# A sparse attention with a mixture of experts: the last 64 keys' products with V on four quarter tiles, no scaling of q on ScalarE, and a new order of all operations, gating and first fetches

## The chip, the cores and the metric

The kernel runs on one NeuronCore of a Trainium2 chip. The metric is the device time of one execution in microseconds. Engines are named as in the profile: PE is TensorE, PEld its weight load, DVE is VectorE, ACT is ScalarE, POOL is GpSimd, SP is SyncE, which issues nearly all DMAs.

## The reference

Attention over 8 batches of 8 heads with 576 positions of 64 elements keeps, in each row, only the scores that lie within tau of the row's maximum. Its output goes through a noisy gate that sends each of 4608 tokens to two of eight experts. All is in 32-bit floats.

```python
scores = q @ k.T / sqrt(64)                       # 576 x 576 for each head
thresh = max(scores, -1) - tau
scores = where(scores >= thresh, scores, -1e9)
attn = exp(scores - max(scores, -1)); attn /= sum(attn, -1) + 1e-9
x = rows of (attn @ v), 4608 x 512
noisy = x @ w_gate + log1p(exp(x @ w_noise)) * noise
two largest of noisy per token -> weights by softmax over the two
out[token] += weight * relu(x @ w1[e]) @ w2[e]    # 512 -> 1024 -> 512
```

## The kernel before

The attention goes by *pairs* of heads, 32 of them, four to a batch; two heads of 64 elements fill the 128 partitions. For a pair there are nine tiles of scores: eight of 128 rows (four for each head) and one, number 0, with the last 64 rows of both heads. A tile passes five stations: `scores` (L305, PE; each operand is split in a high and a low part, hi and lo), `rowmax` (L316, DVE: scores by minus 1/8 to SBUF, with the row's extreme), `exponent` and `threshold` (L322, L330, ACT), `mask` (L344, DVE: keeps what lies under the threshold and adds up the row), `ptile` (L356, PE transposes) and `pcopy` (L364, ACT, PSUM to SBUF). `prem` and `pcorner` turn what belongs to the last 64 keys into the tile ptr.

`avpiece` (L432) multiplies by V. The output of a pair is made in two pieces of 320 and 256 columns (`PIECES`), each in a bank of its own; head s goes to partitions 64 s to 64 s + 63. For keys 0 to 511 a product takes 128 rows and 64 columns of the array, for the last 64 keys (kt = 4) 64 rows and 64 columns. `oev` (L438) copies a piece, `xlpart` (L451, L452) turns it and multiplies it by the gate's weights, `xev` (L465) scales it to xr.

Before its scores a pair's q and k are made ready: `scale_q` (L224, ACT) multiplies q by 1 or 0 as tau is not negative or is, `split` (L234 ACT, L235 POOL) makes hi and lo, and `spread` (L256, SP) copies them within SBUF to where the two heads need them; qd holds the last 64 rows of q (L251, POOL). `norm` and `invert` (L400 to L411) make the reciprocal of the row sums, mostly on POOL.

After every fourth pair comes the *gating* of a batch: `gate_sum` (t, t, lgs on POOL), `gate_abs` (ab, DVE), exponential and logarithm on ACT, `gate_soft` to `gate_soft2` on POOL with one DVE reciprocal, `gate_max` (five maxima and five index searches on DVE), `gate_hot`, `gate_rank` (PE), `gate_slot` and ten `gate_put`, each an indirect DMA of POOL to slot_table. For the last batch but one and the last this runs beside the start of the first expert (`Experts.start`): tokens and index from the table, gathers of rows (L973, POOL), a bounce through DRAM (L983), loads (L993), and the first layers (L1023).

Nothing is reordered on the chip. Each engine runs its instructions in the order in which the program recorded them and waits on semaphores. That order is set by tables of times: `at` files each call under a time, and the calls are then made in order of time. A pair is nine units long. `TIMES` gives each station of a pair its time from the pair's start (S scores, R rowmax, E, H threshold, M mask, T, P, A products with V by piece and key tile, O, X, V; values over 9 fall beside later pairs), `LAST` what differs for the last two pairs, `GATES` and `PUTS` the gating, `START` the first expert. PSUM has two double banks for scores (sp) and four banks (tp) for all else in the attention, taken in turn.

Of the kernel before, what the change touches and what calls it, by code (L numbers as in the profile page):

```python
# [79 lines left out]

TIMES = dict(
    S=(-0.9, 2.24, 2.9, 3.76, 4.09, 5.17, 5.5, 6.47, 8.21),
    R=(-0.03, 2.79, 3.44, 3.87, 4.41, 5.93, 6.26, 7.12, 8.86),
    E=(0.94, 3, 4.74, 6.37, 6.91, 7.02, 9.4, 10.16, 10.38),
    H=(1.27, 0, 4.3, 0, 5.39, 0, 7.45, 0, 9.62),
    M=(1.7, 4.96, 5.06, 6.58, 7.56, 7.88, 9.83, 10.81, 11.68),
    T=(2.14, 5.61, 12.22, 12.33, 13.2, 13.63, 13.85, 15.15, 15.69),
    P=(2.57, 6.8, 13.52, 12.65, 14.28, 14.82, 14.71, 16.23, 16.99),
    A=((17.53, 18.18, 17.32, 18.29, 19.92),
       (19.05, 17.64, 18.08, 17.75, 19.59)),  # L90
    Tc=3.11, Pc=3.98, Tr=15.04, Pr=16.34, O=(20.03, 20.46), X=(26.25, 25.67), V=(27.51, 25.77), norm=11.75, rec=13.9, qs=0.73, hq=1.49, hk=2.35, load=.2)
# [1577 lines left out]
```

## Time and profile before

| | us |
|---|---|
| median of 3 runs | 1484.45 (1484.42 to 1487.59) |
| the profiled execution | 1470.92 |
| its span, first to last instruction | 1469.2 |
| PE busy in the span | 1371.4 (93%) |
| DVE busy | 1061.7 (72%) |
| ACT busy | 845.3 (58%) |
| POOL busy | 750.7 (51%) |
| mean granted TensorE clock | 0.986 |

Busy shares over the whole span mix two programs: up to about 625 us the attention, with its gating, and from there the experts, where DVE and ACT have much less to do. They are read by stage. A pair's place in the trace is found by its first row maximum (L316): the first is at 9.38 us, that of the third pair at 43.54, of the seventh at 110.00, of the thirty-first at 548.28. The gating of the first batch begins just after 110. Matmuls of 32-bit floats appear as two instructions each.

### The profile page before, as it was taken

The page shows a single profiled execution, that of the slowest core. Times are in us where ns is not written, and L with a number is a line of the kernel's source. Part 1 is how long each engine was busy: PE and PEld are TensorE (multiplying, and loading weights), DVE is VectorE, ACT ScalarE, POOL GpSimd, SP SyncE. Part 2 cuts the span into 40 slices and gives each one's busy share as a digit, 9 for nine tenths or more (in the row PEclk, how much of TensorE's full clock was granted, in tenths as well). Part 3 has the DMA queues.
Part 4 walks back from the last instruction along what each step waited for, and adds up shares of the span by engine and source line. Part 5 has one row for each costly group of instructions (what it writes and reads, how often), then busy time and mean ns, then how long its engine had stood idle before and what let it go on. Part 6 is the DMA issues. An engine that isn't in the chain of part 4 may idle for free.

```text
span 1469.2 us, 27611 instructions
## 1 busy us (share of the span) xinstructions
PE 1371.4 (93%) x9086; PEld 1187.4 (81%) x9086; DVE 1061.7 (72%) x2863; ACT 845.3 (58%) x1808; POOL 750.7 (51%) x1149
## 2 busy tenths in 40 slices
PE   6999999999999996888989999999999999999997
PEld 4887777777777775677888898998988988988995
DVE  6998988898988896562675785767766757857740
ACT  5998878887888785431253453445445434534441
POOL 3436665656565656334285455365445544553512
PEclk8999999999999999999999999999999999999998
DMA  6777776777686657245465666475565756564622
GB/s 178 193 192 215 187 203 166 207 189 207 170 213 169 170 151 192 52 96 135 106 176 112 166 136 155 107 172 136 134 127 146 176 100 170 133 156 108 145 30 32
DMA packets 189521, 220.58 MB, mean 150 GB/s; under 512 B 64452, under 2 KB 112540, under 8 KB 188352
## 3 DMA queue, kind: packets, MB, share of 16 engines
q1 hardware_dynamic: 162176, 178.91, 44.2%
q0 software_dynamic: 27200, 39.88, 16.4%
q8 instruction: 73, 1.20, 0.4%
q14 instruction: 72, 0.59, 0.1%
HBM read 103.25 MB, written 60.61 MB: 112 GB/s over the span
## 4 chain that ended last, share of the span: by engine, by line
PE 47%; DVE 18%; issue 12%; ACT 8%; POOL 7%; DMA 5%; SPq 2%; another core or an unknown queue 0%; POOLq 0%; DVEq 0%; ACTq 0%
PE m_tp L1298 13%; PE m_sp L1376 10%; PE sp L305 5%; PE m_tp L1376 5%; DVE p L344 4%; DVE ns L316 4%; PE tp L356 3%; ACT e L322 2%; PE tp L432 2%; PE m_sp L1298 2%; ACT pt L364 2%; PE m_sp L1391 1%; PE m_tp L1391 1%; PE m_tp L1023 1%; SPq L1228 1%
## 5 line engine op out<-in xcount | busy, mean ns | idle before, releaser
L344 DVE SCALAR_TENSOR_TENSOR p<-ns,thr,e 128x576 f32<-128x576 f32 x256 | 235.9, 936 | 7.3 <-ACT e L322 3.8
L322 ACT ACTIVATE e<-ns,nm 128x576 f32<-128x576 f32 x288 | 216.7, 776 | 37.9 <-DVE ns L316 37.8
L316 DVE TENSOR_SCALAR_CACHE_REDUCE ns<-sp 128x576 f32<-128x576 f32 x288 | 207.7, 750 | 23.3 <-PE sp L305 8.1
L1065 POOL DMA_INDIRECT out<-n_y,sx x52 | 85.3, 1641 | 190.2 <-ACT n_y L1367 182.7
L305 PE MATMUL sp<-ks,qh 128*128 128x288 f32 x496 | 155.5, 331 | 24.0 <-DVE ns L316 23.9
L364 ACT ACTIVATE pt<-tp 128x512 f32<-128x512 f32 x256 | 148.5, 595 | 4.7 <-PE tp L356 4.6
L356 PE MATMUL tp<-ident,p 128*128 128x128 f32 x1024 | 141.2, 276 | 3.1 <-DVE p L344 3.0
L305 PE MATMUL sp<-ks,ql 128*128 128x288 f32 x496 | 139.3, 298 | 0.0
L432 PE MATMUL tp<-pt,vt 128*64 128x320 f32 (+1 forms) x1024 | 132.5, 409 | 2.2 <-ACT pt L364 2.0
L356 PEld LDWEIGHTS tp<-ident,p 128*128 128x128 f32 x1024 | 120.8, 143 | 6.8 <-ACT pt L364 3.5
L305 PEld LDWEIGHTS sp<-ks,qh 128*128 128x128 f32 x496 | 95.0, 192 | 37.4 <-DVE ns L316 33.7
L1317 DVE TENSOR_TENSOR n_qr<-m_tp,n_qr 128x320 f32<-128x320 f32 (+1 forms) x154 | 69.7, 459 | 61.1 <-PE m_tp L1298 51.6
L432 PEld LDWEIGHTS tp<-pt,vt 128*64 128x64 f32 x1024 | 73.2, 137 | 48.4 <-issue 3.9
L235 POOL TENSOR_TENSOR loq<-qr,hiq 128x576 fp32r<-128x576 f32 x31 | 46.9, 1513 | 118.7 <-ACT hiq L234 110.0
L1065 POOL DMA_INDIRECT out<-n_y,ix x60 | 96.4, 1607 | 18.6 <-issue 11.9
L1298 PE MATMUL m_tp<-n_p,n_pt 128*128 128x320 f32 (+1 forms) x616 | 101.9, 302 | 3.7 <-ACT n_qr L1314 3.0
L699 POOL DMA_INDIRECT slot_table<-pay,sl x80 | 83.5, 1044 | 33.6 <-issue 28.9
L305 PEld LDWEIGHTS sp<-ks,ql 128*128 128x128 f32 x496 | 95.4, 192 | 0.0
L1298 PEld LDWEIGHTS m_tp<-n_p,n_pt 128*128 128x128 f32 x616 | 89.4, 189 | 6.2 <-ACT n_qr L1314 4.6
L1314 ACT ACTIVATE n_qr<-m_tp 128x320 f32<-128x320 f32 (+1 forms) x140 | 57.6, 413 | 58.8 <-PE m_tp L1298 34.9
L1367 ACT ACTIVATE n_y<-m_sp,gw 128x512 f32<-128x512 f32 (+1 forms) x36 | 24.8, 688 | 97.4 <-PE m_sp L1376 61.9
L1267 ACT ACTIVATE n_vt<-n_qr 128x640 fp32r<-128x640 f32 (+1 forms) x42 | 29.3, 701 | 86.7 <-DVE n_qr L1248 86.7
(615 smaller groups left out, 3976.8 us busy)
## 6 DMA issues: line engine op xcount, KB each, us to landing
qh<-hiq SPq DMA_DIRECT2D x124, 144.0 KB
ql<-loq SPq DMA_DIRECT2D x124, 144.0 KB
n_raw<-w SPq DMA_DIRECT2D x56, 256.0 KB
kr<-k SPq DMA_DIRECT2D x32, 320.0 KB
out<-zeros SPq DMA_DIRECT2D x19, 512.0 KB
qr<-q SPq DMA_DIRECT2D x32, 288.0 KB
vt<-v SPq DMA_DIRECT2D x8, 1152.0 KB
ks<-hik SPq DMA_DIRECT2D x62, 144.0 KB
```

The source lines that it names most:

```text
L305: nc.tensor.matmul(o, q_, k_, start=(i == 0), stop=(i == len(parts) - 1))
L316: nc.vector.tensor_scalar(ns, sp[:, :, 0:HALF], -1.0 / math.sqrt(D), None, op0=ALU.mult, op1=ALU.min, accum_out=nm)
L322: nc.scalar.activation(e, ns, AF.Exp, bias=nm, scale=-1.0)
L344: nc.vector.scalar_tensor_tensor(p, ns, thr, e, op0=ALU.is_le, op1=ALU.mult, accum_out=ssum[n][:, c:c + 1])
L356: nc.tensor.transpose(tp[:, kt, :], p[:, 128 * kt:128 * kt + 128], ident)
L364: nc.scalar.activation(pt[n][:, s, :, c0:c0 + 128], tp, AF.Copy)
L432: nc.tensor.matmul(o[64 * s:64 * s + 64, 0:c1 - c0], w, x, start=(a == 0), stop=(a == 4))
L699: st = nc.gpsimd.indirect_dma_start(out=table, out_offset=bass.IndirectOffsetOnAxis(ap=d["sl"][0:m, i, c:c + 1], axis=0), in_=d["pay"][0:m ...
L1065: st = self.nc.gpsimd.indirect_dma_start(out=out, out_offset=bass.IndirectOffsetOnAxis(ap=idx, axis=0), in_=y, in_offset=None, compute_op= ...
L1298: nc.tensor.matmul(ps[:, 0:n], w[a[0]][hw][:, 128 * (a[1] + c):128 * (a[1] + c) + 128], s[hx][:, c0 + c, t0:t0 + n], start=(first and i == ...
L1317: return lambda: nc.vector.tensor_tensor(to, ps, to, op=ALU.add)
L1376: nc.tensor.matmul(ps[0:m], x[:, col:col + m], y, start=(i == 0 and j == 0), stop=(i == 7 and j == 2))
```

## The change

- `avpiece` puts the second piece of a head on the other half of the partitions, m = 64 (s xor i). With the four products of the last 64 keys one behind the other, each then has a quarter of the array of its own. `oev` copies the second piece back in two instructions.
- `scale_q` is gone; `rowmax` multiplies by a column, scale, that holds minus 1/8 or 0. The column and atau are made after the fetch of the first q and k, and the fetch of tau comes behind theirs. The identity is made before all else.
- The low parts of k and q, with their copies, are calls of their own (`low_k`, `low_q`), with times lk and lq; k comes first.
- `GATES` has a time for each gating operation, one set for most batches and one for the last three; maxima and index searches are filed one by one. Some of the last batch but one goes by `START`.
- `TIMES`, `LAST` and `START` have new numbers throughout.

```diff
-    hq=1.49, hk=2.35, load=.2)
+    'qs': 0.58, 'hq': 1.54, 'hk': 0.48, 'lq': 4.78, 'lk': 3.65, 'load': 0.2}
...
-GATES = (0, 1.6, 2.4, 3.6, 4.4, 4.6, 7, 8.2, 10.74, 11.4, 11.5, 12.3, 12.4, 12.9, 13)
+GATES = ({'sum': 29, 'abs': 32.5, 'exp': 33.5, 'soft': 34.45, 'soft1': 36.3, 'soft2': 36.6, ...
...
+        ident = state["ident"] = const.tile([128, 128], F32, name="ident")
+        make_identity(nc, ident)
...
-        if n == 0:
-            scale_q(0)
...
-    def scale_q(n):
-        qr = raw[n][1]
-        nc.scalar.activation(qr, qr, AF.Copy, scale=scale)
...
+    def low_k(n):
+        hi, lo = st["k", n]
+        nc.gpsimd.tensor_tensor(lo, raw[n][0], hi.bitcast(F32), op=ALU.subtract)
+        spread(n, "ks", [nc.sync])
+
+    def low_q(n):
+        hi, lo = parts = st.pop(("q", n))
+        nc.gpsimd.tensor_tensor(lo, raw[n][1], hi.bitcast(F32), op=ALU.subtract)
+        for t, x in zip(QD, parts):
+            for s in range(2):
+                p = slice(64 * s, 64 * s + 64)
+                nc.gpsimd.tensor_copy(t[p, p], x[p, 512 * (1 - s):512 * (1 - s) + 64])
+        spread(n, "qs", [nc.sync])
...
-        nc.vector.tensor_scalar(ns, sp[:, :, 0:HALF], -1.0 / math.sqrt(D), None, op0=ALU.mult, op1=ALU.min, accum_out=nm)
+        nc.vector.tensor_scalar(ns, sp[:, :, 0:HALF], scale, None, op0=ALU.mult, op1=ALU.min, accum_out=nm)
...
-            nc.tensor.matmul(o[64 * s:64 * s + 64, 0:c1 - c0], w, x, start=(a == 0), stop=(a == 4))
+            m = 64 * (s ^ i)
+            nc.tensor.matmul(o[m:m + 64, 0:c1 - c0], w, x, start=(a == 0), stop=(a == 4))
...
-        nc.scalar.activation(ot[n][:, c0:c1], av.pop((n, i))[0][:, 0:c1 - c0], AF.Copy)
+        o = av.pop((n, i))[0]
+        for a, b in ((0, 128),) if i == 0 else ((0, 64), (64, 128)):
+            m = 64 - a if i else 0
+            nc.scalar.activation(ot[n][a:b, c0:c1], o[m:m + b - a, 0:c1 - c0], AF.Copy)
...
     load(0)
+    tau_b = const.tile([128, 1], F32, name="tau_b")
+    nc.sync.dma_start(tau_b, bass.AP(tensor=tau.tensor, offset=tau.offset, ap=[[0, 128], [1, 1]]))
+    scale = const.tile([128, 1], F32, name="scale")
+    nc.vector.tensor_scalar(scale, tau_b, 0.0, -1.0 / math.sqrt(D), op0=ALU.is_ge, op1=ALU.mult)
...
-            at(g + d["hq"], None, spread, n + 1, "qs", [nc.sync])
+            at(g + d["lq"], None, low_q, n + 1)
```

The order of PE around the products with V of the fifth pair, before; pt holds the probabilities of keys 0 to 511, ptr those of the last 64:

```order
L452 MATMUL tp_1578<-xl,ot_1393 128x2x16
L432 MATMUL tp_1583<-pt_1140,vt_573 64x320 x4
L432 MATMUL tp_1588<-pt_1140,vt_573 64x256 x6
L432 MATMUL tp_1583<-pt_1140,vt_573 64x320 x4
L432 MATMUL tp_1588<-pt_1140,vt_573 64x256 x2
L432 MATMUL tp_1588<-ptr_1141,vt_573 64x256 x2
L432 MATMUL tp_1583<-ptr_1141,vt_573 64x320 x2
L356 MATMUL tp_1660<-ident,pr_1651 128x128 x4
```

And now:

```order
L459 MATMUL tp_1576<-ident,ot_1395 64x2x64
L460 MATMUL tp_1576<-xl,ot_1395 64x2x16
L437 MATMUL tp_1583<-ptr_1188,vt_567 64x320 x2
L437 MATMUL tp_1587<-ptr_1188,vt_567 64x256 x2
L437 MATMUL tp_1583<-pt_1187,vt_567 64x320 x2
L437 MATMUL tp_1587<-pt_1187,vt_567 64x256 x6
L437 MATMUL tp_1583<-pt_1187,vt_567 64x320 x4
L437 MATMUL tp_1587<-pt_1187,vt_567 64x256 x2
L437 MATMUL tp_1583<-pt_1187,vt_567 64x320 x2
L304 MATMUL sp_1642<-ks_1350,qh_118 128x288
```

The four products with ptr stood last, two for one piece and two for the other, and now stand first, with the second piece on the other partitions.

The order of POOL for the preparation of the sixth pair (hik, hiq and the low parts) beside the normalizer of the fourth (ssum, rn), before:

```order
L235 TENSOR_TENSOR loq_1115<-qr_837,hiq_1114 128x576
L251 COPY qd_129<-hiq_1114 64x64 x2
L251 COPY qd_130<-loq_1115 64x64 x2
L235 TENSOR_TENSOR lok_1154<-kr_836,hik_1153 128x640
L400 TENSOR_SCALAR ssum_875<-ssum_875 128x9
L407 COPY rn_1230<-ssum_875 128x4
L408 COPY rn_1230<-ssum_875 64x1
L409 COPY rn_1230<-ssum_875 64x4
```

And now:

```order
L229 TENSOR_TENSOR lok_1097<-kr_829,hik_1096 128x640
L404 TENSOR_SCALAR ssum_880<-ssum_880 128x9
L234 TENSOR_TENSOR loq_1118<-qr_830,hiq_1117 128x576
L238 COPY qd_122<-hiq_1117 64x64 x2
L238 COPY qd_123<-loq_1118 64x64 x2
L411 COPY rn_1252<-ssum_880 128x4
L412 COPY rn_1252<-ssum_880 64x1
L413 COPY rn_1252<-ssum_880 64x4
```

lok now comes first, and loq with its copies to qd behind the first operation of the normalizer, which needs the last mask of the pair before.

DVE at that place now; ssum_880 is the pair whose normalizer POOL takes there, ssum_1137 the next:

```order
L315 TENSOR_SCALAR ns_1157,nm_1158<-sp_1124,scale 128x576
L315 TENSOR_SCALAR ns_1166,nm_1158<-sp_1130,scale 128x576
L343 SCALAR_TENSOR_TENSOR p,ssum_880<-ns_1120,thr_1033,e_1135 128x576
L343 SCALAR_TENSOR_TENSOR p,ssum_1137<-ns_1157,thr_1159,e_1169 128x576
L315 TENSOR_SCALAR ns_1212,nm_1213<-sp_1176,scale 128x576
L315 TENSOR_SCALAR ns_1222,nm_1213<-sp_1182,scale 128x576
L343 SCALAR_TENSOR_TENSOR p,ssum_1137<-ns_1166,thr_1159,e_1224 128x576
```

Behind the last mask of the older pair stand a mask of the next, two row maxima and a mask.

POOL where the first expert's gathers begin, beside the gating sums (t, t, lgs) of the seventh batch, before:

```order
L973 DMA m_y_8214<-x_rows,sx_74 128x512
L973 DMA m_y_8271<-x_rows,sx_74 128x512
L973 DMA m_y_8214<-x_rows,sx_74 128x512
L565 TENSOR_TENSOR t_8346<-xr_134 128x320
L568 TENSOR_TENSOR t_8348<-t_8346 128x160
L570 TENSOR_TENSOR lgs_8350<-t_8348 128x80
L235 TENSOR_TENSOR loq_8377<-qr_8063,hiq_8376 128x576
L251 COPY qd_129<-hiq_8376 64x64 x2
L251 COPY qd_130<-loq_8377 64x64 x2
L235 TENSOR_TENSOR lok_8423<-kr_8062,hik_8422 128x640
```

And now:

```order
L1006 DMA m_y_8275<-x_rows,sx_79 128x512
L1006 DMA m_y_8314<-x_rows,sx_79 128x512
L573 TENSOR_TENSOR t_8362<-xr_127 128x320
L576 TENSOR_TENSOR t_8364<-t_8362 128x160
L578 TENSOR_TENSOR lgs_8366<-t_8364 128x80
L1006 DMA m_y_8275<-x_rows,sx_79 128x512
L1006 DMA m_y_8314<-x_rows,sx_79 128x512
L229 TENSOR_TENSOR lok_8334<-kr_8055,hik_8333 128x640
L404 TENSOR_SCALAR ssum_8106<-ssum_8106 128x9
```

The sums stood behind the third gather and now stand ahead of it; the third and the fourth gather stand ahead of lok, and loq further down.

## Rows read from the trace of the kernel before

**Rows 1.** Stages: us; busy us of PE, PEld, DVE, ACT, POOL; PEclk, DMA, GB/s.
```profile
...
60.17:76.78 16.61, 16.61 (x136) 13.81 (x134) 15.44 (x43) 15.05 (x32) 6.42 (x12) 1.00 0.72 187
110.00:129.22 19.22, 18.71 (x152) 15.06 (x150) 17.52 (x62) 15.40 (x34) 12.98 (x26) 1.00 0.86 239
...
200.59:220.61 20.02, 17.94 (x142) 14.16 (x140) 15.85 (x47) 15.12 (x33) 13.41 (x29) 1.00 0.72 179
110.00:548.28 438.28, 412.28 (x3255) 334.55 (x3253) 388.07 (x1110) 363.14 (x786) 275.80 (x536) 1.00 0.72 187
548.28:726.20 177.92, 147.38 (x845) 124.33 (x842) 98.85 (x322) 61.88 (x131) 73.75 (x114) 0.94 0.51 124
726.20:1469.20 743.00, 716.54 (x4296) 650.05 (x4295) 484.47 (x1190) 334.07 (x712) 361.45 (x404) 0.99 0.56 129
```

**Rows 2.** Chain of waits, 40 to 120 us: start, length, engine, what.
```profile
...
59.42 5.15 PE tp L432 x40
...
76.04 5.15 PE tp L432 x40
...
81.77 1.07 PE sp L305 x8
```

**Rows 3.** Waits, 110 to 548 us: who for whom, us in total, times, longest.
```profile
...
PEld tp L356 <- DVE pr L344: 18.8, 17, 1.7
...
DVE gq L672 <- POOL gs L657: 9.8, 6, 1.6
```

**Rows 4.** Timeline of one undisturbed pair: start, us, engine, line, operation.
```profile
...
59.35 4.10 PE L432 MATMUL tp<-pt,vt 128*64 128x320 f32 x32
...
60.47 0.76 ACT L224 ACTIVATE qr<-qr,scale 128x576 f32<-128x576 f32 x1
...
63.38 1.19 PE L432 MATMUL tp<-ptr,vt 64*64 64x256 f32 x8
...
63.52 0.81 DVE L344 SCALAR_TENSOR_TENSOR p<-ns,thr,e 128x576 f32<-128x576 f32 x1
...
64.12 1.49 POOL L235 TENSOR_TENSOR loq<-qr,hiq 128x576 fp32r<-128x576 f32 x1 [9.46 <-ACT hiq L234]
...
64.26 1.97 DVE L344 SCALAR_TENSOR_TENSOR p<-ns,thr,e 128x576 f32<-128x576 f32 x1
...
64.50 0.66 PE L356 MATMUL tp<-ident,pr 128*128 128x128 f32 x4
...
65.58 0.38 ACT L438 ACTIVATE ot<-tp 128x256 f32<-128x256 f32 x1
...
66.16 0.75 DVE L316 TENSOR_SCALAR_CACHE_REDUCE ns<-sp 128x576 f32<-128x576 f32 x1
...
67.26 1.57 POOL L235 TENSOR_TENSOR lok<-kr,hik 128x640 fp32r<-128x640 f32 x1
...
67.39 2.48 SPq L256 DMA_DIRECT2D ql<-loq  x4
```

**Rows 5.** Costliest groups: busy us, mean ns of one, idle before.
```profile
...
L432 PE MATMUL tp<-pt,vt 128*64 128x320 f32 (+1 forms) x1024 | 132.5, 409 | 2.2 <-ACT pt L364 2.0
```

**Rows 6.** Timeline of VectorE in the first gated pair.
```profile
...
114.67 1.41 DVE L577 SCALAR_TENSOR_TENSOR ab<-lgs 128x40 f32<-128x40 f32 x1 [0.24 <-POOL lgs L570]
```

**Rows 7.** Timeline of the first 12 us.
```profile
...
2.20 0.43 SPq L213 DMA_DIRECT2D qr<-q  x1
...
4.02 4.18 PE L192 MATMUL tp<-ident 128*128 128x128 f32 x20 [4.02 <-POOL ident masks.py:199]
...
6.66 0.78 ACT L224 ACTIVATE qr<-qr,scale 128x576 f32<-128x576 f32 x1 [0.75 <-DMA qr<-q]
...
8.13 1.19 PE L294 MATMUL sp<-kr,qr 64*64 64x288 f32 x8
```

**Rows 8.** Timeline of GpSimd where the first expert's gathers begin.
```profile
...
554.68 0.95 POOL L973 DMA_INDIRECT m_y<-x_rows,sx  x1 [8.88 <-issue]
```

**Rows 9.** Waits of TensorE, 548 to 726 us.
```profile
...
PE sp L305 <- DVE ns L316: 8.7, 3, 5.2
```

More of the change, by code (lines that the diff above doesn't have):

```diff
@@ L357, in ptile, with turned @@
         st["t", n, j] = tp
+    def turned(n):
+        if n not in pt:
+            pt[n] = rot(work, [128, 2, 4, S], F32, name="pt")
+            ptr[n] = rot(work, [128, 640], F32, name="ptr")
     def pcopy(n, j):
+        turned(n)
         tp = st.pop(("t", n, j))
@@ L615, in gate_max, with gate_max1, gate_index @@
         d["ix"] = small([NB, 8], U32, "ix")
-        for i in range(NB):
-            vec.max(d["mx"][:, i, :], d["nl"][:, i, :])
-        for i in range(NB):
-            vec.max_index(d["ix"][:, i, :], d["mx"][:, i, :], d["nl"][:, i, :])
+    def gate_max1(b, i):
+        d = gt[b]
+        vec.max(d["mx"][:, i, :], d["nl"][:, i, :])
+    def gate_index(b, i):
+        d = gt[b]
+        vec.max_index(d["ix"][:, i, :], d["mx"][:, i, :], d["nl"][:, i, :])
     def gate_hot(b):
@@ L751, in attention, with stage @@
                 at(g + x, 5, bump)
-            for i, (to, f) in enumerate(zip(GATES, (
-                    gate_sum, gate_abs, gate_exp, gate_soft, gate_soft1, gate_soft2, gate_max, gate_hot, gate_rank,
-                    gate_rank1, gate_slot, gate_slot1, gate_pay, gate_slot2, gate_slot3))):
-                at(G + START["gate"][STAGES[i]] if late else g + x + to, 5 if late else 0, f, b)
+            times = GATES[b >= B - 3]
+            def stage(c, f, i=None):
+                to = times[c] if i is None else times[c][i]
+                if late or (b == B - 2 and STAGES[c] > 6):
+                    at(G + START["gate" if late else "gate0"][STAGES[c]], 5, f, b, *([] if i is None else [i]))
+                    return
+                at(g + to, 0, f, b, *([] if i is None else [i]))
+            for c, f in (("sum", gate_sum), ("abs", gate_abs), ("exp", gate_exp), ("soft", gate_soft), ("soft1", gate_soft1),
+                         ("soft2", gate_soft2), ("soft2", gate_max)):
+                stage(c, f)
+            for c, f in (("max", gate_max1), ("index", gate_index)):
+                for i in range(NB):
+                    stage(c, f, i)
+            for c, f in (("hot", gate_hot), ("rank", gate_rank), ("rank1", gate_rank1), ("slot", gate_slot),
+                         ("slot1", gate_slot1), ("pay", gate_pay), ("slot2", gate_slot2), ("slot3", gate_slot3)):
+                stage(c, f)
             for i in range(2 * NB):
-                to = g + x + PUTS[i]
+                to = g + times["put"][i]
                 if experts and b >= B - 2:
```

71 lines of the change are left out of this document (22 added, 49 removed), and 20 rows, old and new, of tables (LAST, START, TIMES).

## The prediction

> **What bounds the kernel now.** I read the stage table first, then the chain of waits, then one undisturbed pair of heads, then the waits of the gated stretch. In [rows 1] a pair without gating work takes 16.61 us, and TensorE is busy through all of it, VectorE for 15.44, ScalarE for 15.05: TensorE is the bound, the others are 1.2 to 1.6 us behind. The chain shows the same: one pair's products with V begin at 59.42, the next's at 76.04, 16.62 apart, 5.15 of it for these products [rows 2]. The third row of [rows 1] is another sort of pair: 20.02 us, TensorE busy for 17.94. From 110.00 to 548.28 there are 24 pairs in 438.28 us, 18.26 each, so 1.65 over the undisturbed pair, or 6.6 us for each batch of four (438.28 / 6 = 73.05 against 4 x 16.61 = 66.44). In that stretch TensorE waits for masks of VectorE, while VectorE itself waits for small gating results of GpSimd [rows 3]. Behind the attention come 177.92 us in which the first expert starts, TensorE busy for 147.38 at a clock of 0.94, and 743.00 us of experts, which the change leaves as they are.
>
> **The change part by part.** *Quarter tiles.* In a pair's products with V the 32 instructions over 512 keys start at 59.35 and the eight over the last 64 keys at 63.38; the next transposes start at 64.50 [rows 4]. Two run at once (one of the two heads on each half of the columns): 16 steps in 4.03 us are 0.252 each for 288 columns on average, and four steps of the last 64 keys by that rate 1.01, which with 0.11 for the change of tile shape is the 1.12 seen. Overlap is also plain in the group's row: 1024 instructions of 409 ns in 132.5 us [rows 5]. With four at once, two steps of 320 columns are left, 2 x 0.252 x 320 / 288 = 0.56: 0.45 us less a pair. Four at once is not in this trace. The bounds are 0 (they still go two by two) and 0.45; no shape change is added (there is one into the quarter tiles and one out of them, before and now), so I see no loss. I take 0.45, since the two streams of one row group, which is what is new, already run side by side in the 128-row tiles of [rows 4]. The group now stands first, before the products that need the last transposed copy, which only loosens that edge.
>
> The Trainium skill speaks against this (TensorEngine Tiling (Array Packing), Restrictions and Gotchas, PSUM Pressure): different row tiles cannot access one PSUM bank at the same time. By that rule nothing is gained here, and the time would be 14 us above my forecast. But the eight of [rows 4] are two row tiles writing the two halves of one bank, and they take the time of two at once; so the trace disagrees where it can be asked.
>
> *The scaling of q* goes from ScalarE: 0.76 us of instruction [rows 4], some 0.67 of its time. The copy of the second piece of the output becomes two of 64 partitions: 0.38 now, and a second of 0.20 (the smallest copies here are 64 x 64) to 0.38. ScalarE falls from 15.05 to about 14.7; TensorE at 16.1 hides either. The row maximum takes its factor from a pointer: its price is not in the trace. A mask, which has a pointer, shows 0.81 against 0.75 for the row maximum [rows 4]; so between 0 and 9 x 0.06 = 0.54 us of VectorE a pair. I take 0, because a mask also has a second tensor; VectorE's reserve covers either.
>
> *The two low parts on GpSimd.* At 64.12 GpSimd starts loq, which reads two tensors, and the mask that starts at 64.26 ends only after it: the next VectorE instruction starts at 66.16, 1.90 later, against 0.74 from the mask before to this one [rows 4]. That is 1.16 us a pair. lok at 67.26 falls on row maxima, which are not held. In the new order loq stands behind the normalizer of the pair before, thus behind that pair's last mask; one mask and two row maxima follow there. So it falls mostly on row maxima, and I expect VectorE's need to fall from 15.44 to about 14.3 to 14.6. On an undisturbed pair this is worth nothing by itself (TensorE bounds it), but it is the reserve out of which gating is paid.
>
> *Undisturbed pairs*: 16.61 - 0.45 = 16.16, and some 0.1 of small waits may go: 16.1. Four of them (pairs 2 to 5): 2 us.
>
> *Gated pairs.* The gating operations are the same in number, but each stands far behind the one that feeds it, and the first pair of a batch no longer takes them all. VectorE's extra work is what the first gated pair has over an undisturbed one, 17.52 - 15.44 = 2.1 us [rows 1], and half a microsecond in the others; its waits for GpSimd, such as the 9.8 us for one reciprocal [rows 3] and the 0.24 before a 40-element operation that then lasts 1.41 beside GpSimd [rows 6], go. Also the first transposes of a pair move from right behind their mask to a third of a pair after it; that edge cost 18.8 us in 17 waits [rows 3]. VectorE now needs 4 x 14.5 + 2.6 = 60.6 a batch, TensorE 4 x 16.1 = 64.4. What is left over TensorE lies between 0 (all covered) and the 6.6 of now. I take 2, nearer to nothing, because the reserve, 3.8 us, is more than the work put in. That makes 66.4 a batch, 6 x (73.05 - 66.4) = 40 us less. With all waits left it would be 24 x 0.45 = 11, with none 52.
>
> *Start.* The identity is made first and q and k are fetched before tau. Now the ten warming products run from 4.02 to 8.2 and the first scores at 8.13 [rows 7]. A q issued at 2.20 was there at 6.66, 4.5 later; k of the first pair, issued at about 1.3 instead of 1.74, lands by 5.8; the warming I put 2.5 us earlier, as GpSimd's index fills no longer stand before the identity, so it is over by then. So 2.3 us, in bounds of 0 and 3.
>
> *The start of the first expert.* GpSimd's third gather waits 8.88 us for a buffer [rows 8], and behind it stand the gating sums, for them VectorE, for that TensorE: 5.2 us [rows 9]. The sums now stand before that gather. But two gathers now stand in front of lok and loq of the last pair, and the rest of this order is new too. I take 5 us gained, between 15 gained (half of the 30.5 TensorE is idle there) and 10 lost.
>
> **The sum** against the profiled execution (1470.92 us): 2 + 40 + 2.3 + 5 = 49.3, so 1421.6. The runs' median, 1484.45, is 13.5 above that execution for the same kernel; I take the same gain off it: 1435 us.
>
> **The rivals.** *Two by two.* The quarter tiles don't overlap: 32 x 0.45 = 14 us are missing, 1449. For: four at once is nowhere in the trace. Against: two streams and two row groups each run at once. *Late low parts.* Before, the four ql copies were issued from 67.39 to 69.87 [rows 4], and the scores that need them come at 81.77, behind the next products with V [rows 2]. Moving loq behind the last mask takes three or four of these 12 us (81.77 - 69.87), the landing of a copy as much again, and the gating sums and the puts, a microsecond or more each, now stand in front of it on GpSimd. Where the copies come late, scores wait: at 1 us a gated pair 24 us of the gain go, 1459. *Masks held twice.* If lok meets a mask as loq does now, each pair pays 1.16 + 1.3 on VectorE; with 14.3 of need, the 2.6 a batch of gating, and a microsecond of waits a pair for thresholds, that is 18.4 a pair, more than the 18.26 of now, and VectorE bounds the undisturbed pairs too (17.8 x 4, 5 us lost). With 3 lost over the gated pairs, 2.3 won at the start, and the expert's start losing 2 instead of gaining, the kernel is slower: about 1492. It decides once VectorE's need passes TensorE's present 16.6. Against it: in the new order lok's input is copied by ScalarE just before row maxima, not before masks.
>
> **How the numbers follow.** The forecast, 1435, has its own range of 1418 to 1450 and a chance of 0.60; two by two 0.08; late low parts, or another wait that takes the place of those removed, 0.22; held masks 0.06; and 0.04 that gains and losses cancel. The range that should hold the time 8 times in 10 goes from 1412 (all gating waits gone, 52, and 15 gained at the expert's start) to 1466, a little past late low parts. A measurement of this kernel tells 0.3%, 4.5 us, from no change; so faster 0.90, same 0.03, slower 0.07.
>
> **What would show it.** Right: undisturbed pairs at 16.1 to 16.2; the eight instructions of the last 64 keys in about 0.7 us with the shape change; no mask of 1.9 us in an ordinary pair; gated batches near 66; TensorE's waits for pr masks gone; first scores near 6 us. Wrong: scores that wait for copies of ql; masks beside lok; pairs still at 19 to 20 us where the gating sums run; or a longer stretch between the last pair and the experts, as the order there is wholly new.

## The result, and the profile after

| | before | after |
|---|---|---|
| median of 4 runs each, us | 1484.79 (1484.42 to 1487.59) | 1443.61 (1440.72 to 1445.19) |
| ratio of after to before | | 0.972, 95% interval 0.970 to 0.974 |
| the profiled execution's span, us | 1469.2 | 1438.8 |

The kernel is 41 us faster by the medians, 30.4 by the two traces; why these differ is told at the end of the account of the prediction. The stages of the trace after, cut at the same places as [rows 1], with the pair in which slot numbers are written as the last row (columns as there: stretch, its length, busy time of the engines, granted clock, DMA):

```profile
62.33:78.28 15.95, 15.95 (x136) 13.48 (x134) 15.55 (x41) 14.91 (x33) 6.36 (x12) 1.00 0.71 181
110.19:527.73 417.54, 402.75 (x3256) 328.17 (x3254) 384.71 (x1112) 364.40 (x787) 276.77 (x537) 1.00 0.76 196
527.73:693.50 165.77, 145.40 (x833) 124.12 (x830) 92.63 (x319) 62.22 (x131) 74.44 (x113) 0.93 0.54 134
693.50:1438.80 745.30, 716.89 (x4297) 651.44 (x4295) 484.49 (x1188) 334.75 (x712) 369.51 (x404) 0.99 0.55 129
177.45:196.02 18.57, 17.41 (x132) 13.52 (x129) 15.75 (x45) 14.89 (x34) 14.67 (x30) 1.00 0.83 208
```

Against [rows 1] that is, in us:

| stage | before | after | change | predicted |
|---|---|---|---|---|
| start to the fourth pair's first row maximum | 60.17 | 62.33 | +2.2 | -2.3 |
| three undisturbed pairs | 49.83 | 47.86 | -2.0 | -2 (for four) |
| 24 gated pairs | 438.28 | 417.54 | -20.7 | -40 |
| last pairs and start of the first expert | 177.92 | 165.77 | -12.2 | -5 |
| experts | 743.00 | 745.30 | +2.3 | 0 |
| sum | 1469.2 | 1438.8 | -30.4 | -49.3 |

An undisturbed pair after, in order of time (start, duration, engine, line, operation). L437 is the product with V, L315 the row maximum, L343 the mask, L229 and L234 the low parts of k and q:

```profile
60.86 0.76 PE L437 MATMUL tp<-ptr,vt 64*64 64x320 f32 x8
61.54 4.10 PE L437 MATMUL tp<-pt,vt 128*64 128x320 f32 x32
...
62.39 1.55 POOL L229 TENSOR_TENSOR lok<-kr,hik 128x640 fp32r<-128x640 f32 x1 [4.25 <-DMA ql<-loq]
...
63.07 1.49 DVE L343 SCALAR_TENSOR_TENSOR p<-ns,thr,e 128x576 f32<-128x576 f32 x1
...
69.63 1.43 POOL L234 TENSOR_TENSOR loq<-qr,hiq 128x576 fp32r<-128x576 f32 x1
...
70.11 0.81 DVE L315 TENSOR_SCALAR_CACHE_REDUCE ns<-sp,scale 128x576 f32<-128x576 f32 x1
```

The eight products of the last 64 keys take 0.68 us (60.86 to 61.54) where [rows 4] had 1.12. The mask of 1.97 us beside loq is gone: loq now lies beside row maxima, which are not held (0.81). But lok, which lay beside row maxima, now meets the mask at 63.07, and that one takes 1.49. So one long mask was exchanged for a shorter one.

The waits from 110 to 528 (who waited for whom, us in total, times, longest). TensorE's 18.8 us for masks of the remainder tile and VectorE's 9.8 for gs [rows 3] are not among them any more; what is left around the transposes and the scores is small:

```profile
PEld sp L304 <- DVE ns L315: 9.8, 27, 1.0
...
POOL pay L693 <- DVE gq L684: 8.2, 5, 1.6
...
PEld tp L352 <- ACT pt L366: 3.4, 10, 0.5
```

Yet one pair of each batch is long, 18.1 to 19.6 us, the others 16.2 to 17.1 until pair 25 (counted from 0). GpSimd in that pair, whose products with V begin at 176.07 (L711 writes slot numbers, L573 is the first gating sum):

```profile
176.95 0.96 POOL L711 DMA_INDIRECT slot_table<-pay,sl  x1 [0.23 <-issue]
...
178.21 1.62 POOL L711 DMA_INDIRECT slot_table<-pay,sl  x1 [0.21 <-issue]
...
181.12 0.86 POOL L573 TENSOR_TENSOR t<-xr 128x320 f32<-128x320 f32 x1
...
184.14 1.57 POOL L229 TENSOR_TENSOR lok<-kr,hik 128x640 fp32r<-128x640 f32 x1
...
187.27 1.43 POOL L234 TENSOR_TENSOR loq<-qr,hiq 128x576 fp32r<-128x576 f32 x1
```

Seven writes in a row, the first at 172.94, and the sums stand in front of lok, which starts 8.1 us after the pair's products with V; in the undisturbed pair it is 0.85 (62.39 against 61.54).

### The profile page after: what moved, and what is told of

The parts are those of the page before. It is cut to its first block, busy times and chain, and to the rows that moved or that the text cites. A ratio compares the mean times of both kernels' runs of the same rounds, so it can differ in the third digit from the quotient of the medians.

```text
span 1438.8 us, 27655 instructions
## 1 busy us (share of the span) xinstructions
PE 1364.0 (95%) x9086; PEld 1184.9 (82%) x9086; DVE 1053.8 (73%) x2863; ACT 846.2 (59%) x1808; POOL 761.5 (53%) x1148
## 3 DMA queue, kind: packets, MB, share of 16 engines
q1 hardware_dynamic: 162176, 178.91, 45.2%
## 4 chain that ended last, share of the span: by engine, by line
PE 61%; DVE 12%; issue 8%; ACT 6%; DMA 6%; POOL 4%; SPq 2%; POOLq 0%; DVEq 0%; ACTq 0%
PE m_tp L1331 13%; PE m_sp L1409 9%; PE tp L437 8%; PE sp L304 7%; PE tp L352 5%; PE m_tp L1409 5%; PE m_sp L1056 3%; PE m_sp L1077 2%; DVE ns L315 2%; DMA n_zeros<-stage 2%; PE m_sp L1331 2%; DVE p L343 2%; POOL out L1098 1%; PE m_tp L1056 1%; DVE n_pt L1217 1%
## 5 line engine op out<-in xcount | busy, mean ns | idle before, releaser
L321 ACT ACTIVATE e<-ns,nm 128x576 f32<-128x576 f32 x288 | 221.9, 777 | 34.1 <-DVE ns L315 26.2
L315 DVE TENSOR_SCALAR_CACHE_REDUCE ns<-sp,scale 128x576 f32<-128x576 f32 x288 | 224.9, 809 | 20.8 <-PE sp L304 13.0
L343 DVE SCALAR_TENSOR_TENSOR p<-ns,thr,e 128x576 f32<-128x576 f32 x256 | 225.0, 886 | 15.5 <-ACT e L321 14.3
L366 ACT ACTIVATE pt<-tp 128x512 f32<-128x512 f32 x256 | 142.8, 598 | 23.1 <-PE tp L352 21.5
L437 PE MATMUL tp<-pt,vt 128*64 128x320 f32 (+1 forms) x1024 | 134.1, 409 | 1.7 <-issue 1.7
L437 PEld LDWEIGHTS tp<-pt,vt 128*64 128x64 f32 x1024 | 71.9, 137 | 60.0 <-issue 18.3
L711 POOL DMA_INDIRECT slot_table<-pay,sl x80 | 91.7, 1146 | 20.5 <-issue 13.2
L1331 PEld LDWEIGHTS m_tp<-n_p,n_pt 128*128 128x128 f32 x616 | 89.3, 189 | 10.5 <-ACT n_qr L1347 10.2
L1331 PE MATMUL m_tp<-n_p,n_xr 128*128 128x320 f32 (+1 forms) x308 | 72.8, 301 | 2.4 <-ACT n_qr L1347 2.4
```

The source lines that it names most:

```text
L315: nc.vector.tensor_scalar(ns, sp[:, :, 0:HALF], scale, None, op0=ALU.mult, op1=ALU.min, accum_out=nm)
L321: nc.scalar.activation(e, ns, AF.Exp, bias=nm, scale=-1.0)
L343: nc.vector.scalar_tensor_tensor(p, ns, thr, e, op0=ALU.is_le, op1=ALU.mult, accum_out=ssum[n][:, c:c + 1])
L366: nc.scalar.activation(pt[n][:, s, :, c0:c0 + 128], tp, AF.Copy)
L437: nc.tensor.matmul(o[m:m + 64, 0:c1 - c0], w, x, start=(a == 0), stop=(a == 4))
L711: st = nc.gpsimd.indirect_dma_start(out=table, out_offset=bass.IndirectOffsetOnAxis(ap=d["sl"][0:m, i, c:c + 1], axis=0), in_=d["pay"][0:m ...
```

## The experiments

In the table and in the expectations the attention is cut at the first product with V (512 keys) of pairs 2, 5 and 28, counted from 0, and the experts at the first product of the first expert's second layer (693.5 us after, 726.0 before). The columns: time as a ratio to the kernel before, run on the same chip, with its interval; an undisturbed pair (pair 2 to pair 3); the four steps from pair 15 to pair 19, as many as a batch has; pair 5 to pair 28; pair 28 to the second layer. All in us, from one trace each. The runs were on three chips (the kernel before took 1486.4, 1448.5 and 1479.9 us on them), so times are compared through the ratio, and the stages through the traces: the attention has the same length on all three, the experts do not (733 to 734 us in the runs no_puts to late_k0, 743 to 747 in the others).

| run | ratio | undisturbed | pairs 15 to 19 | 5 to 28 | 28 to 2nd layer |
|---|---|---|---|---|---|
| before | 1 | 16.61 | 17.29 17.38 20.08 18.41 | 420.9 | 178.6 |
| after | 0.972 (0.970-0.974) | 15.96 | 16.21 19.13 16.26 17.03 | 400.7 | 166.7 |
| half | 0.979 (0.975-0.982) | 16.39 | 16.38 19.25 16.68 17.44 | 405.4 | 165.6 |
| early_k | 0.971 (0.968-0.975) | 15.95 | 16.21 19.31 16.27 17.02 | 403.1 | 165.3 |
| exp_scale | 0.973 (0.971-0.976) | 16.03 | 17.82 18.93 16.19 17.15 | 405.5 | 167.9 |
| old_gates | 0.976 (0.973-0.978) | 15.96 | 16.37 17.59 17.83 17.18 | 403.8 | 167.4 |
| no_puts | 0.975 (0.972-0.978) | 15.96 | 15.95 16.62 16.29 17.01 | 384.8 | 163.9 |
| early_lk | 0.981 (0.978-0.984) | 15.96 | 15.95 19.09 16.75 17.02 | 398.0 | 165.1 |
| old_low | 1.019 (1.016-1.022) | 16.56 | 16.50 24.67 17.67 17.75 | 447.8 | 164.4 |
| late_k0 | 0.979 (0.976-0.982) | 15.97 | 16.22 18.20 16.77 17.03 | 396.6 | 164.4 |
| const_scale_early_k | 0.972 (0.970-0.974) | 15.96 | 16.85 18.85 16.04 16.88 | 397.0 | 168.0 |
| paced | 0.968 (0.966-0.970) | 15.96 | 16.50 16.35 17.07 17.02 | 389.8 | 166.6 |
| before_quarter | 1.000 (0.998-1.003) | 16.62 | 17.29 17.38 20.07 18.37 | 422.3 | 185.9 |
| old_start | 0.985 (0.983-0.987) | 15.96 | 16.22 19.09 16.27 17.01 | 404.7 | 178.5 |

**Quarter tiles: half and before_quarter.**

```diff
 half, from the kernel after
-            m = 64 * (s ^ i)
+            m = 64 * s
-            m = 64 - a if i else 0
+            m = a
```

> Two quarter tiles undone: the second piece's products go back to the same half of the columns as the first piece's; its copy stays in two halves and the order stays. Theory (four run at once): the eight instructions of the last 64 keys took 0.68 us in the changed kernel (60.86 to 61.54) and 1.12 before, so 0.44 a pair comes back; an undisturbed pair goes from 15.96 to 16.4, and with 32 pairs the time rises by 6 to 14 us, 1450 to 1458 (the lower end if VectorE, not TensorE, holds the gated pairs). Rival (two by two, the gain came from the new order alone): the pair stays at 15.96 and the time within 2 us of 1443.6.

TensorE in the run half, last 64 keys and what follows:

```profile
61.20 1.19 PE L437 MATMUL tp<-ptr,vt 64*64 64x320 f32 x8
62.31 4.10 PE L437 MATMUL tp<-pt,vt 128*64 128x320 f32 x32
```

1.11 us instead of 0.68, and the undisturbed pair 0.43 longer. Four products do run at once, and *two by two* has fallen. Of the 23 pairs from 5 to 28 only some take the 0.43 on: 4.7 us in all, 0.2 a pair. The time is 0.7% more by the ratios, some 10 us, as the theory had it.

before_quarter puts the same tiles, and the output copy in halves, into the kernel before:

```diff
+            m = 64 * (s ^ i)
-            nc.tensor.matmul(o[64 * s:64 * s + 64, 0:c1 - c0], w, x, start=(a == 0), stop=(a == 4))
+            nc.tensor.matmul(o[m:m + 64, 0:c1 - c0], w, x, start=(a == 0), stop=(a == 4))
```

> The kernel before with the four quarter tiles alone (its order, its scaling of q and its gating times stay). Theory (the gain exists only where TensorE bounds a pair): undisturbed pairs 16.61 to 16.4 or 16.2, as VectorE, with its mask of 1.97 us, needs 15.44 and stands close behind; from pair 5's products with V to pair 28's 414 to 421 instead of 420.9; the time 2 to 8 us less than before. Rival 1 (all 32 pairs give 0.44): 14 us less. Rival 2 (nothing, the pairs being held by other waits): within 2 us.

Its time is that of the kernel before to 0.3%. The last 64 keys do take less, and the time is lost again within the pair. TensorE (L433 products with V, L305 scores) in an undisturbed pair of this run:

```profile
85.87 0.77 PE L433 MATMUL tp<-ptr,vt 64*64 64x256 f32 x8
86.57 0.66 PE L356 MATMUL tp<-ident,pr 128*128 128x128 f32 x4
...
89.47 0.40 PE L305 MATMUL sp<-ks,qh 128*128 128x288 f32 x1 [0.18 <-DVE ns L316]
```

and VectorE beside it (L344 the mask, L316 the row maximum):

```profile
86.75 1.98 DVE L344 SCALAR_TENSOR_TENSOR p<-ns,thr,e 128x576 f32<-128x576 f32 x1
...
88.66 0.75 DVE L316 TENSOR_SCALAR_CACHE_REDUCE ns<-sp 128x576 f32<-128x576 f32 x1
```

The eight end at 86.57, 0.70 after their start, and then the scores at 89.47 wait for a row maximum that stands behind the mask held by loq. They start 3.60 us after the eight. In the kernel before, where the eight start at 63.38 [rows 4], it is 3.59:

```profile
66.97 0.40 PE L305 MATMUL sp<-ks,qh 128*128 128x288 f32 x1
```

So by these scores nothing is left of what the eight gained. Rival 2 was right. Together with half this is a table of two by two for the undisturbed pair: 16.61 with neither part, 16.62 with the quarter tiles alone, 16.39 with the rest of the change alone, 15.96 with both.

**VectorE's load: early_k, exp_scale, const_scale_early_k.**

```diff
 early_k
-    0.58, 'hq': 1.54, 'hk': 0.48, 'lq': 4.78, 'lk': 3.65, 'load': 0.2}
+    0.58, 'hq': 1.54, 'hk': 0.45, 'lq': 4.78, 'lk': 3.65, 'load': 0.2}
 exp_scale
-    nc.vector.tensor_scalar(scale, tau_b, 0.0, -1.0 / math.sqrt(D), op0=ALU.is_ge, op1=ALU.mult)
+    nc.vector.tensor_scalar(scale, tau_b, 0.0, -1.0, op0=ALU.is_ge, op1=ALU.mult)
-        nc.vector.tensor_scalar(ns, sp[:, :, 0:HALF], scale, None, op0=ALU.mult, op1=ALU.min, accum_out=nm)
+        nc.vector.tensor_scalar(ns, sp[:, :, 0:HALF], -1.0 / math.sqrt(D), None, op0=ALU.mult, op1=ALU.min, accum_out=nm)
-        nc.scalar.activation(e, ns, AF.Exp, bias=nm, scale=-1.0)
+        nc.scalar.activation(e, ns, AF.Exp, bias=nm, scale=scale)
 const_scale_early_k: hk as in early_k, the row maximum as in exp_scale, the exponential as before
```

> One ScalarE instruction of each pair, the high part of k, is moved one place up, in front of an exponential that is not needed for 3 us; so GpSimd's low part of k should run from 61.6 to 63.1 beside two row maxima instead of 62.4 to 63.9 beside a mask. Theory (VectorE's need holds the gated pairs): the mask of 1.49 us goes back to 0.81, 0.68 a pair; undisturbed pairs stay at 15.96, the 23 gated pairs, 17.42 each, fall by 0.35 to 0.68, so 8 to 16 us: 1428 to 1436. Rival (the gated pairs are held by waits along the chain of scores, masks and copies, whatever VectorE's load): the mask is short again but the time stays within 3 us of 1443.6.

> The row maximum takes its factor as a constant again; what the pointer did (switching the scores off for a negative tau) moves to the scale of ScalarE's exponential and to a threshold that lets everything pass. Theory (VectorE's need): the row maximum falls from 0.81 to 0.75, nine of them 0.54 a pair; the gated pairs fall by 0.25 to 0.54, 6 to 12 us: 1431 to 1437. Rival 1 (waits, not load): within 3 us of 1443.6. Rival 2 (a pointer costs ScalarE what it cost VectorE, 0.06 by nine exponentials, and ScalarE takes over): no gain, or up to 5 us lost.

> VectorE is made lighter by both of its new charges: the row maximum has a constant factor (the switching off for a negative tau is left out), and the high part of k is one place earlier, so that the low part falls on row maxima; 0.54 + 0.68, some 1.2 us a pair. Told by the trace, from pair 5's products with V to pair 28's, 400.7 us in the changed kernel. Theory of the prediction (gating is paid out of VectorE's reserve): 12 to 25 us less there, 376 to 389. Rival (GpSimd's slot writes and single waits make the gated pairs long): 396 to 403, and an undisturbed pair at 15.95 as before.

An undisturbed pair of early_k, then of const_scale_early_k (the third busy time is VectorE's):

```profile
76.70:92.65 15.95, 15.95 (x136) 13.49 (x134) 14.88 (x41) 14.88 (x34) 6.36 (x12) 1.00 0.77 196
```

```profile
80.53:96.48 15.95, 15.95 (x136) 13.49 (x134) 14.55 (x41) 14.86 (x34) 6.57 (x12) 1.00 0.73 196
```

VectorE's need did fall, from 15.55 to 14.88 and 14.55, and the time did not: 5 to 28 moved by +2.4 and -3.7 us, where a reserve that pays for gating would have given 12 to 25. That theory has fallen. exp_scale was no clean test, as its second rival came true: with a column as its factor the exponential itself takes 0.877 us instead of 0.777 (mean of 288), ScalarE's need goes from 14.91 to 15.57, and another pair of the batch becomes 17.8.

**The gating times: old_gates.** The five first batches get the distances of the kernel before:

```diff
-GATES = ({'sum': 29, 'abs': 32.5, 'exp': 33.5, 'soft': 34.45, 'soft1': 36.3, 'soft2': 36.6, 'max': (38.3, 38.8, 39.3,
+GATES = ({'sum': 27.75, 'abs': 29.35, 'exp': 30.15, 'soft': 31.35, 'soft1': 32.15, 'soft2': 32.35, 'max': (34.75, 34.75, 34.75, 34.75, 34.75),
...
```

> The gating operations of the five first batches stand at the distances of the kernel before (all behind the batch's last pair, the five maxima and indices together, the whole set in one and a half pairs) in the otherwise changed order. Theory (their spreading over four pairs is what the gated pairs gained): a batch goes from 69 us back towards 73, 2 to 4 us in each of five batches, so 10 to 20 us: 1454 to 1464. Rival (the gain came from the order inside the pair and from the quarter tiles): less than 4 us, 1443 to 1448.

5 to 28 grows by 3.1 us, the time by 0.4%: the rival. The long pair is shorter (17.59; the writes are then elsewhere), and the next one is longer (17.83 instead of 16.26). Spreading the gating was not what the gated pairs gained by.

**The slot writes: no_puts, early_lk, paced.**

```diff
 no_puts
-                at(to, 5, gate_put, b, i // 2, i % 2)
+                if b >= 5:
+                    at(to, 5, gate_put, b, i // 2, i % 2)
 early_lk
-    0.58, 'hq': 1.54, 'hk': 0.48, 'lq': 4.78, 'lk': 3.65, 'load': 0.2}
+    0.58, 'hq': 1.54, 'hk': 0.48, 'lq': 4.78, 'lk': 0.9, 'load': 0.2}
 paced: hk 0.45, lk 0.9, and in the first set of GATES
-'put': (56.15, 56.9, 57.4, 61.2, 61.9, 62.2, 63.3, 64, 64.3, 65.4)
+'put': (56.15, 56.2, 56.25, 61.5, 62.2, 65.2, 65.5, 73.2, 73.5, 73.8)
```

> The ten indirect writes of token slots per batch are left out for the five first batches (the experts then gather default rows for them). In the changed kernel one pair of each batch of four is long, 18.1 to 19.6 us against 16.0 to 17.1 of the others, and in it GpSimd issues six of these writes and the gating sums in front of the low part of k, which starts 7 us later than elsewhere. Theory (GpSimd's writes make that pair long): it falls to 16.3 to 17, 2 to 3 us in each of five batches, 1429 to 1434. Rival (VectorE's need, or the gating operations themselves): that pair stays over 18 and the time within 3 us of 1443.6.

> The low part of k is put in front of the slot writes and the gating sums in GpSimd's order (it needs only the high part, which is there); in pairs without them nothing changes. Theory 1 (the lateness of the low parts and of the copies behind them makes the long pair): the long pair of a batch falls by 1 to 2.5 us, six batches, 1430 to 1438. Theory 2 (the writes themselves hold the other engines while they are issued, wherever the low part stands): within 3 us of 1443.6.

Without the writes the long pair is 16.62 instead of 19.13, and 5 to 28 falls by 15.9. The four pairs sum to 65.9, where the prediction had 66.4 for a batch. (On its chip no_puts has a ratio of 0.975, early_lk 0.981; the ratio of the kernel after was measured on another, so these say little of the two by themselves, and the same holds for the 0.979 of late_k0.) Moving lok alone gave 2.7 us of these. Where it did not help, one pair of 20.86 us, the rows of early_lk show why. Copies of q's high part from SP's queue, four in a row:

```profile
181.66 7.01 SPq L255 DMA_DIRECT2D qh<-hiq  x4
```

then the corners of q on GpSimd, and the scores that need them on TensorE:

```profile
191.90 0.46 POOL L238 CAST qd<-hiq 64x64 fp32r<-64x64 f32 x1 [2.16 <-issue]
```

```profile
192.41 0.40 PE L304 MATMUL sp<-hik,qd 128*128 128x288 f32 x1 [1.75 <-POOL qd L238]
```

In an undisturbed pair these four copies are issued in 2.48 us, here in 7.01. Most of that is one wait before the fourth, which the profile puts down to a DMA and not to GpSimd:

```profile
SPq L255 <- DMA vt<-v: 4.4, 1, 4.4
```

GpSimd's second small copy stands still for 2.16 us, for nothing that the profile names, and TensorE waits 1.75 for it. So lok alone is not what is late: here it is the corners of q, which stand behind the writes on GpSimd as well. That the bunch of writes holds them is argued from this pair; the next run tests it.

> The low part of k ahead of GpSimd's slot writes, the high part of k one place earlier, and the ten slot writes of each of the five first batches no longer in a row of six but three, two, two and three, each right behind the low part of k or behind the last small copies of a pair. Theory (the bunched writes delay GpSimd's small copies of q, for which TensorE waits 1.8 us in the run with the early low part): the long pair falls from 18 to 20 us to under 17.3, and from pair 5's products with V to pair 28's it takes 386 to 393 us instead of 400.7, 0.5 to 1% off the time. Rival (each write costs its quarter of a microsecond wherever it stands): 396 to 401, the long pair's excess spread over three pairs.

The long pair is gone (16.50, 16.35, 17.07, 17.02), and 5 to 28 is 389.8, the middle of what was expected, with the same ten writes a batch. Against early_lk, which has lok at the same early place, that is 8.2 us less. The rival had 396 or more. At 0.968 (0.966 to 0.970) against 0.972 (0.970 to 0.974) it is the fastest version here that computes everything; the intervals touch, the two ran on different chips, and the trace says 10.9 us for the stage.

**The low parts: old_low.**

```diff
-    0.58, 'hq': 1.54, 'hk': 0.48, 'lq': 4.78, 'lk': 3.65, 'load': 0.2}
+    0.58, 'hq': 1.54, 'hk': 0.48, 'lq': 1.541, 'lk': 0.481, 'load': 0.2}
```

> Both low parts stand on GpSimd right behind their high parts again, as in the kernel before; the rest of the change stays. By the prediction's term (a mask held by the low part of q, 1.16 us a pair of VectorE's reserve) the gated pairs grow by 0.3 to 1 us, 7 to 20 us in all: 1450 to 1464. Rival 1 (VectorE's load decides in one pair of four only, as the two runs with a lighter VectorE say): 0 to 5 us more, 1443 to 1449. Rival 2 (what counts is that the low parts stand ahead of the slot writes): 2 to 10 us less.

1.9% slower than the kernel before on its chip, so far beyond every case put down. VectorE in an undisturbed pair has two long masks, one beside lok and one beside loq:

```profile
84.67 1.49 DVE L343 SCALAR_TENSOR_TENSOR p<-ns,thr,e 128x576 f32<-128x576 f32 x1
...
86.16 1.89 DVE L343 SCALAR_TENSOR_TENSOR pr<-ns,thr,e 128x576 f32<-128x576 f32 x1
```

and the stages show VectorE busy through nearly all of the undisturbed pair (16.42 of 16.56) and the pair with the writes at a lower clock:

```profile
83.14:99.70 16.56, 16.56 (x136) 13.48 (x134) 16.42 (x41) 14.88 (x34) 6.97 (x12) 1.00 0.72 193
186.92:213.38 26.46, 18.63 (x137) 15.92 (x135) 15.17 (x43) 16.73 (x37) 18.02 (x35) 0.81 0.63 172
```

What makes that pair long is a wait of VectorE, with all its row maxima queued behind it:

```profile
DVE ab L585 <- POOL spacer L710: 8.0, 1, 8.0
PE sp L304 <- DVE ns L315: 7.8, 1, 7.8
```

ab needs the gating sums, and these now stand behind loq and the writes on GpSimd. So the times of the change belong together; one row of the table put back costs 47.1 us from 5 to 28, more than the whole change brings.

**The start: late_k0.**

```diff
-            at(g + d["hk"], None, split_k, n + 1)
+            at(g + (d["hk"] if n else 3.6), None, split_k, n + 1)
```

> In the first pair alone the high part of the next k is put behind the first exponentials on ScalarE. In the changed kernel ScalarE waits 7.07 us for that k, until 9.16, with the first exponential queued behind it, which could start at 8.4. Theory (this wait ate the earlier first scores): the first mask comes 1.4 us earlier, at 9.9 instead of 11.35, and the first products with V at 43.5 to 44 instead of 45.15; the time falls by 1 to 2 us. Rival (the first two pairs are held by the first 8 slow score products and by VectorE): the products with V start within 0.4 of 45.15, and the time is the same.

The first mask came at 9.44 instead of 11.35, as expected, but the products with V at 45.92 instead of 45.15, which neither theory has. The stretches of the first 40 us in which the granted clock stays at one level say more. Run late_k0:

```profile
5.36:12.19 6.83, 5.20 (x27) 3.18 (x26) 4.03 (x12) 2.68 (x5) 0.58 (x5) 1.00 0.65 244
12.19:29.26 17.07, 16.06 (x51) 11.26 (x49) 10.61 (x24) 6.37 (x15) 4.89 (x6) 0.50 0.54 133
```

The kernel after:

```profile
5.52:12.34 6.82, 3.96 (x20) 2.07 (x19) 2.82 (x11) 2.16 (x4) 2.95 (x7) 1.00 0.66 246
12.34:19.17 6.83, 6.45 (x21) 3.81 (x21) 4.45 (x12) 3.72 (x9) 2.44 (x5) 0.50 0.76 178
...
26.00:29.41 3.41, 3.41 (x16) 3.24 (x15) 0.48 (x2) 0.52 (x1) 0.00 (x0) 0.50 0.92 328
...
32.82:39.65 6.83, 5.77 (x24) 5.46 (x25) 5.89 (x16) 4.97 (x11) 3.60 (x6) 0.50 0.57 132
```

The kernel before:

```profile
12.34:24.65 12.31, 9.63 (x47) 5.99 (x45) 9.98 (x27) 6.75 (x15) 3.32 (x6) 1.00 0.65 151
24.65:34.89 10.24, 5.48 (x25) 5.41 (x26) 5.64 (x14) 6.08 (x11) 4.75 (x7) 0.50 0.61 175
```

Before, TensorE has the full clock (2.4 GHz) until 24.65 and half of it for 10.2 us; after, it falls to half at 12.34, once the engine has done its first products and stands for 3 of 6.8 us, and is there for 17.1 of the first 40 us. In late_k0 it is half for 17 us in a row, and later for 6.8 more. That needs no earlier start: before_quarter, whose instructions up to its first products with V are those of the kernel before, is at half clock for 27.3 us,

```profile
12.01:39.31 27.30, 20.15 (x62) 13.49 (x63) 15.61 (x41) 12.37 (x27) 6.63 (x11) 0.50 0.48 126
```

and its first products with V come at 47.54, where the kernel before has 41.99. The runs half, old_gates, no_puts and old_start, with the first instructions of the kernel after, have 20.5, 17.1, 13.7 and 23.9 us at half clock. Over all fourteen traces the first products with V go with that time: 42.0 with 10.2 us at half clock, 43.4 with 13.7, 44.2 to 45.2 with 17.1, 45.9 to 46.8 with 20.5 to 23.9, and 47.5 to 49.1 with 27.3. So executions with the same first instructions differ in this stage by more than the change was to gain there. What decides the granted clock no run shows, and one trace each can't tell what the earlier first scores are worth.

**The expert's start: old_start.** The table START of the kernel before, with the gating of the last batch but one filed at the same place:

```diff
-START = {'raw': (-21.3, -21.45, -12.45), 'tok': -29.5, 'ix': -20.9, 'ga': (-20.3, -19.2, -17.1), 'ba': (-18.9, -18.3,
+START = dict(
+    raw=(-21, -21, -12), tok=-28, ix=-24, ga=(-23, -21, -20), ba=(-21, -20, -18), la=(-19, -17, -16), ta=(-12, -11, -8),
...
```

> The changed kernel with the times of the kernel before for the first expert's start (gathers, first layer, last batch's gating and slot writes). From pair 28's products with V to the first product of the second layer that follows the first expert (693.5) the changed kernel takes 166.7 us, the kernel before 178.6. Theory (the new start times gain these 11.9): 174 to 180, the time 8 to 13 us more. Rival (the gain there comes from the last pairs of the attention, lighter on TensorE and with less gating in front): 165 to 170, within 3 us.

Its stage, and the time 1.3% more:

```profile
531.51:710.00 178.49, 149.87 (x839) 126.21 (x838) 98.70 (x322) 63.44 (x134) 73.98 (x114) 0.90 0.49 120
```

178.5 is what the kernel before takes, and before_quarter, with the same times, takes 185.9; the eleven kernels with the new times take 163.9 to 168.0. The whole gain of that stage comes from the new start times.

## Why the prediction was right, step by step

The forecast was 1435 in a range of 1412 to 1466 (the terms named for the lower end add up to 1413); 1443.6 came. Direction and range were right, for reasons that hold only in part, and with some luck.

- **Quarter tiles.** The size was right: 0.45 forecast, 0.44 by the trace, 0.43 by half. The Trainium skill's rule that different row tiles can't use one PSUM bank at the same time (TensorEngine Tiling (Array Packing), Restrictions and Gotchas, PSUM Pressure) doesn't hold here: the eight write two halves of each of two banks in 0.68 us. What failed is the step "TensorE is the bound" for the undisturbed pair of the kernel before: before_quarter shows a second path of the same length through the held mask. The forecast of 16.1 was close to 15.96 because the change cuts both paths.
- **VectorE's need.** Forecast 14.3 to 14.6, measured 15.55. Two terms were off: the column as factor cost its upper bound (row maximum 0.750 to 0.809 us, nine a pair, 0.54), taken as 0; and lok fell on a mask after all, 0.68. 15.44 - 1.16 + 0.68 + 0.54 = 15.50. The Trainium skill has the mechanism (SBUF - State Buffer, SBUF: two separate sides): an operation of VectorE with two inputs in SBUF and one of GpSimd that reads SBUF exclude each other. The traces agree for masks beside lok and loq (1.49 and 1.89 to 1.98 us) and for row maxima, which read PSUM (0.81 beside loq).
- **Gated pairs.** This is the step that failed: -40 forecast, -20.7 measured. An undisturbed pair gained 0.66; the same over 24 pairs would be 15.8 of the 20.7. What a gated pair takes beyond an undisturbed one hardly fell: 1.65 us before, 1.45 after (417.54 / 24 - 15.95), where the forecast had 0.5. VectorE's reserve was not what paid (const_scale_early_k), and the spreading of the gating was not the gain (old_gates, 3 us). The waits named did go, and with the slot writes left out a batch takes 65.9. What the forecast left out is one pair per batch with a bunch of writes in front of the low parts and of the corners of q, 2.5 us each. The rival *late low parts* named the place, sums and puts on GpSimd in front of the preparation of q and k, but not the wait: scores that wait for copies of ql are not among the waits of the trace after, and lok alone was worth 2.7 us. It was priced over all gated pairs, 24 us; the writes cost 16 in one of four (five batches). Which waits make the long pair of the kernel after is not shown step by step; that the bunched writes do is (no_puts, paced).
- **What did bring the 20.7.** Quarter tiles 4.7 by half, gating times 3.1 by old_gates; that leaves 12.9, by subtraction and not by a run, for the order inside the pair, the low parts included, and for what ScalarE no longer does (scale_q was not put back by itself). These parts were not told apart, as old_low shows that one of them put back alone breaks another.
- **Masks held twice.** Its mechanism is real: old_low has it, with VectorE at 16.42 in a pair, close under the 16.6 from which the prediction let it decide; the long pair of that run, though, came from the late gating sums.
- **Start.** -2.3 forecast, +2.2 measured. The first scores begin at 5.80, as forecast,

```profile
5.80 1.62 PE L293 MATMUL sp<-kr,qr 64*64 64x288 f32 x9
```

and the first row maximum is 1.7 us earlier (7.65 against 9.36, where the section on the time before has 9.38). What failed is the step from there to the end of the stage: the forecast carried the 2.3 us on unchanged, and the first products with V move by more than that from one execution to the next, along with the granted clock. The +2.2 is against an execution with little half clock; against before_quarter the first products with V come 2.4 us earlier (45.15 and 47.54). So this term is neither confirmed nor refuted.
- **The expert's start.** -5 forecast, -12.2 measured, near the 15 put as its bound, all of it from START (old_start). The term was too small, as a guess between wide bounds.
- **From trace to median.** The forecast took the same 13.5 us between profiled execution and median for both kernels; after, it is 2.9. These 10.6 us helped the forecast, and they are luck: by the traces alone 30.4 of the forecast 49.3 us came. The profiled execution of before, 1470.92, is faster than all 24 runs in which that kernel was timed outside the chip of no_puts (1474.94 to 1488.39). before_quarter, with the same code at the start and at the expert's start and the same median time, reaches pair 5 at 132.5 instead of 126.6 and takes 185.9 instead of 178.6 to the second layer, 13 us in just these two stages; it is at half clock for 27.3 and 34.1 us in them, the trace of before for 10.2 and 20.5. A second trace of the kernel before itself was not taken.

## What to carry to other kernels

A gain on the busiest engine counts only if no second path of the same length runs beside it: look for the wait that would come next before a saved half microsecond is multiplied by the number of pairs. Where small jobs share an in-order queue with copies that the next round needs, keep them from bunching in front of those copies; spreading ten writes, with the low part of k ahead of them, gained two thirds of what leaving them out did (10.9 of 15.9 us). Where the clock enters a stage, one trace of each kernel is not enough to price a change of a few microseconds there. A table of times is tuned as a whole, so undoing one entry measures the clash it makes, not what that entry brought.

## What the runs showed of the hardware that was not expected

- A column as factor costs both engines on 128x576 tiles, against a constant: VectorE's row maximum 0.809 against 0.750 us, ScalarE's exponential 0.877 against 0.777.
- Behind a bunch of GpSimd's indirect writes a 64x64 copy of GpSimd stood still for 2.16 us (early_lk). The same ten writes a batch, spread out, cost 5.0 us from pair 5 to pair 28 (389.8 against 384.8 without them), and bunched 15.9.
- With the same first instructions TensorE was at half clock for 10.2 us of the start in one execution and for 27.3 in another (before, before_quarter).
- The same kernel took 1448.5 us on one chip and 1480 to 1486 on two others; in the traces the attention is equally long on all three, and the experts take 733 to 734 us instead of 743 to 747. That is 11 us of some 35; the kernel before was not traced on the fast chip, so where it saves the rest is not known.
